# Turning eight half batches by transposing DMAs in a linear-attention and routed-MLP kernel

## The chip, the cores and the metric

The kernel runs on one core of one Trainium2 chip. The metric is the device time of that core in microseconds, the median of several runs. Before the change it is 963.09 us (three runs, 963.00 to 963.91). The profiled execution has a span of 960.4 us at a granted TensorE clock of 1.00.

## The reference

Two stages follow each other. Linear attention over 8 batches, 8 heads, 576 tokens and a head size of 64:

```python
q_p, k_p = phi(q), phi(k)                      # phi(x) = elu(x) + 1
kv  = einsum('bhsd,bhse->bhde', k_p, v)
z   = sum(k_p, axis=2)
num = einsum('bhsd,bhde->bhse', q_p, kv)
den = einsum('bhsd,bhd->bhs', q_p, z)[..., None] + 1e-6
x   = (num / den)                              # then laid out as 4608 tokens x 512
```

Then a routed MLP on x with 8 experts, hidden size 1024:

```python
P = exp(x @ w_gate);  eight times: normalise rows, then columns (Sinkhorn)
out = sum over e of  P[:, e:e+1] * (relu(x @ w1[e]) @ w2[e])
```

Every expert sees every token, so the two matmuls per expert are nearly all of the arithmetic.

## The kernel before

**Stages.** The front computes attention. The work is cut into 16 *half batches* n = 2b + g: batch b, four of its eight heads. The function `att(b, g)` makes the tasks of one. The result is `xT`, the attention output with features on the partitions and tokens along the free axis, as the first MLP layer needs it. The MLP is cut into units of 512 tokens (g = 0 to 8) per expert e. For expert 0, units 0 to 4 are plain (`layer1` at L583 for `hq`, `unit_plain` at L809 for `ye`), and units 5 to 8 have a first layer of seven block products instead of eight (`block7`, matmuls at L703). Experts 1 to 7 use seven-product forms for both layers (L703, L927). Those begin near 193 us and are the rest of the span.

**One half batch.** k, q and v come by DMA (L269). ScalarE takes the exponential (L285), VectorE makes phi in two steps (L298, L301) into the tile `t`, and v is cast to fp16 beside a column of ones (`f_v`, L229 or L231). TensorE forms k^T v and the sum of k in the PSUM tile `kv_ps` (18 matmuls, L330), whose buffer is single (`p_kv`). It is masked into `kvz` (L341 or L343). q is transposed by TensorE (`qt_ps`, L358) and copied (`qpT`). Then the denominators (`den_ps`, 10 small matmuls, L373), `rden` (an addition and a reciprocal, L379 and L381), the numerators (`num_ps`, L397), their product with the reciprocals (`xn`, three VectorE instructions, L402), two times five TensorE transposes (`xt_ps`, L413) and two copies of 128 x 576 from PSUM into `xT`. `qt_ps`, `den_ps`, `num_ps`, `xt_ps`, the gate's logits and one of the block products share the two PSUM buffers `att`. `xn` has two buffers.

**What waits for the front.** `logits` (L432) needs `xT` of two batches and starts the Sinkhorn rounds, whose P is first needed to finish unit 8 of expert 0. At the end of the front its SBUF and PSUM are closed (`f_close`) and given to what follows: the weight combinations `W` of `block7` (VectorE, L867), the blocks `xst` and the loads `xs` (L653). An instruction on the new tiles waits for the last reader of the old ones. Blocks of x are stored to DRAM for the later experts (`x_blocks`, stores at L606, L607, L636).

**What sets the order.** Every engine runs its instructions in program order. That order is made by the class `_Plan`, a list scheduler: each task has engines with a cost in us, dependences, buffers it takes and a priority, and is emitted when its planned start comes. The priorities are overwritten by a long table of ranks by task number (L1084 on), some of which also pin a task to an engine. A DMA is planned as a task on its issuing engine and one on a single `dma` engine, with a latency of 2.6 us after it. The front runs interleaved with the plain units of expert 0. At the very start 47 warm-up matmuls (L505) fill TensorE.

Of the kernel before, what the change touches and what calls it, by code (L numbers as in the profile page):

```python
# [10 lines left out]
FP32 = mybir.dt.float32  # L11
FP16 = mybir.dt.float16
# [110 lines left out]
def kernel(  # L123
# [10 lines left out]
    nc = tc.nc  # L134
# [34 lines left out]
    NX = 5  # L169
    MG = 99  # L170
# [19 lines left out]
    p_vv, p_kvz, p_qpT, p_xn, p_rden = (S_.pool(2) for _ in range(5))  # L190
# [47 lines left out]
    gates = {}  # L238
    v_land, kv_id = [], []
# [6 lines left out]
    def att(b, g):  # L246
# [67 lines left out]
        def f_v(e):  # L314
            copy(e, gvv["tile"][:, :, :, 0:D], gin["v"]["tile"])
        tvv.append(fadd({"act": 1.15, "dve": 0.76}, f_v, deps=[ta, tin["v"]],
                        use=[gvv, gin["v"]], prio=pr))
# [49 lines left out]
        gden, grd, gxn = S_.grp(p_att), S_.grp(p_rden), S_.grp(p_xn)  # L367

        def f_den(_):
            gden["tile"] = aps.tile([P, 5, 2, 2], FP32, tag="att", name="den_ps")  # L370
            for i, j in enumerate(js):
                for hh in range(2):
                    nc.tensor.matmul(gden["tile"][:, i, :, hh],  # L373
                                     lhsT=gq["tile"][:, hh, j:j + 2, :].rearrange("p j w -> p (j w)"),
                                     rhs=gz["tile"][:, hh, :, D], start=True, stop=True)

        def f_rd(_):
            grd["tile"] = fp.tile([P, 5, 4], FP32, tag="rden", name="rden")
            nc.vector.tensor_scalar(out=grd["tile"], in0=gden["tile"].rearrange("p i r h -> p i (r h)"),  # L379
                                    scalar1=1e-6, scalar2=None, op0=ALU.add)  # L380
            nc.vector.reciprocal(grd["tile"], grd["tile"])  # L381
        tden = fadd(("pe", 0.26), f_den, deps=tq + tz, acq=[gden], use=[gq, gz], prio=pr)
        trd = fadd(("dve", 0.5), f_rd, deps=[tden], acq=[grd], use=[gden], prio=pr)

        def f_xa(_):
            gxn["tile"] = fp.tile([P, 5, 4, D], FP16, tag="xn", name="xn")
        txa = fadd(("none", 0.0), f_xa, deps=[tden], acq=[gxn], prio=pr)
        txn = []
        for i0, i1 in ((0, 2), (2, 4), (4, 5)):
# [11 lines left out]
            def f_xn(_, i0=i0, i1=i1, gn=gn):  # L401
                nc.vector.tensor_tensor(  # L402
# [4 lines left out]
        for c2 in range(2):  # L407
            gx = S_.grp(p_att)

            def f_xt(_, c2=c2, gx=gx):  # L410
                gx["tile"] = aps.tile([P, S], FP16, tag="att", name="xt_ps")
                for i in range(5):
                    nc.tensor.transpose(gx["tile"][:, 64 * js[i]:64 * js[i] + P],  # L413
                                        gxn["tile"][:, i, 2 * c2:2 * c2 + 2, :].rearrange("p r e -> p (r e)"), ident)

            def f_xc(e, c2=c2, gx=gx):
                copy(e, xT[:, 2 * g + c2, S * b:S * b + S], gx["tile"])
            t1 = fadd(("pe", 0.3), f_xt, deps=txn, acq=[gx], use=[gxn], prio=pr)
            xt_done[(b, 2 * g + c2)] = fadd({"act": 0.64, "dve": 0.46}, f_xc, deps=[t1], use=[gx], prio=pr)
# [5 lines left out]
    def logits(b2):  # L425
# [11 lines left out]
        t1 = lg_pe[b2] = add(("pe", 1.0), f_l, deps=[xt_done[(b, c)] for b in (2 * b2, 2 * b2 + 1) for c in range(NDT)],  # L437
# [74 lines left out]
    for i in range(34):  # L512
        twa = add(("pe", 0.3), lambda e, n=2 if 4 <= i < 17 else 1: f_warm(e, n), deps=[twa], use=[gyw], prio=900.0, after=1.2 + 0.5 * i)
# [46 lines left out]
    def layer1(e, g):  # L560
        gw1, tw1, gw2, tw2 = w_t[e]
        bs = range(512 * g // S, (512 * g + 511) // S + 1)
        xd_ = [xt_done[(b, c)] for b in bs for c in range(NDT)]
# [34 lines left out]
    def x_blocks(g):  # L598
        bs = range(512 * g // S, (512 * g + 511) // S + 1)
        deps = [xt_done[(b, c)] for b in bs for c in range(NDT)]  # L600
# [420 lines left out]
    for tt in (3, 2, 1, 0):  # L1021
# [5 lines left out]
        0:-50.0024 36:8.7509 38:8.7566 40:-50.0207 42:-49.9982 43:8.7608 44:-50.0228 45:8.7578 46:-50.0192  # L1027
        47:-50.0138 49:8.7452:act 50:-49.9982 51:-50.0108 52:-50.0204:act 54:8.7572 55:-50.0216 56:8.7563
        57:-49.9985:act 58:-50.0222 59:-50.0213 61:-50.0117 62:-50.0036 63:-50.012 64:8.759 65:-50.0135
        66:-98.0291 67:-50.012 68:8.7602:dve 69:-49.9994 70:-50.0129:act 71:-50.015 73:-50.0144 75:-49.9886  # L1030
        77:-50.0129 78:-49.9988 79:-50.0186 80:8.7587 81:-50.0207 82:-50.0027 84:-50.0198 85:-49.9829
        86:-49.9985:act 88:-98.021 89:-50.015:act 90:-50.0201 91:8.7617:dve 92:-50.0195 93:-50.0219
        95:-50.0162 96:8.7575 97:-50.0201 98:-50.0186 99:8.7464 100:-98.0051 101:-50.0195 102:-50.0144:act
        103:-50.0141 104:-50.0198 106:8.7632 108:8.7575 110:-49.9844 112:-50.0216 114:-50.0006 116:8.7575
        117:-50.0132 118:-50.0006 119:-50.021 120:-50.0192 121:-49.9982 123:-50.0201:dve 124:-50.0159
        125:-50.0225:dve 127:-50.0138 128:-50.0105:dve 129:8.762 130:-50.0213 131:-98.0054 132:-50.0189
        134:-49.9787 135:-50.0207 136:-49.9859 137:-50.003 138:-50.0018 139:-50.0228 140:-50.0153
        141:-50.0093:dve 142:-49.9811 143:-50.0003:dve 144:-50.0156 146:-50.012 148:-50.0147 150:-50.0237
        151:-50.021 152:8.7593 153:-50.0204 154:-50.0192 155:-50.0156 157:-50.0003:act 158:-50.0159
        159:8.7368:dve 161:-50.0117 162:-50.0147:act 163:-50.0021 164:-50.0213 165:-50.0222 166:8.7443  # L1040
        168:-50.021 169:-50.0231 170:-50.0168 171:-50.0267 172:-50.0216 173:-50.0144 174:-50.0228
        175:-50.0228:dve 176:-50.0201 177:-49.9787:act 179:-50.0063 181:-50.006 183:-50.0144 184:-50.0189
        185:-50.0189 187:-50.0168 189:-50.0048 191:8.7584 192:-49.9802 193:-50.0225 194:-50.0255
        195:-50.0201 196:-50.0219 198:-50.0195 199:-50.0132 200:-50.0207:dve 202:-50.0249 203:-50.0144
        204:-50.0015 205:-50.0213:dve 206:-98.0237 207:-50.012 209:-50.0183 210:-50.0204 211:-50.0258
        212:-50.0288 213:-50.0189 214:-50.0237 215:-49.9808 216:-49.9856:act 217:-50.0219 218:-50.0117:dve
        219:8.7602 221:-50.0153 223:-49.9991 225:-50.0015 226:-50.0165 227:-50.0225 228:-50.0162
        229:-98.0078 230:-50.0165 232:-50.0087:dve 233:-98.0054 234:8.7512:dve 236:-50.0216 237:-98.0051:act
        238:-50.0246 239:-50.0165:dve 240:-50.0219 241:-98.0048 243:-50.027 244:-50.0195 245:-50.0135
        246:-50.0126 247:-50.0228 248:-50.0123 249:-50.0159 250:-50.018:act 251:-98.0228 252:-49.9826  # L1050
        253:-50.018 255:-50.0213 257:-50.018 259:-50.0162 260:-50.0231 261:-98.0063 262:-50.0282 263:-50.012
        264:-50.0003 266:-50.0117:dve 267:-50.0159 268:8.7464:act 270:-50.0195 271:8.7509:act 272:-98.0054
        273:-50.0168 274:-50.0162 275:-98.0246 277:-50.015 278:-50.0213 279:-50.0243 280:-50.0273
        281:-50.0174 282:-98.0231 283:-98.003 284:-50.0198:act 285:-98.0261 286:-50.0228:dve 287:-98.0048
        289:-49.9814 291:-49.9808 293:-50.0267 294:-49.9856 295:-50.0282 296:-50.0045 297:-50.0243
        298:8.7446 300:-49.9805 301:-50.0276 302:-50.0186:dve 304:-50.0204 305:-50.0123:act 306:-50.0132
        307:-98.006:act 308:-50.0207 309:-50.0219 311:-49.9784 312:-50.0192 313:-50.0189 314:-50.0123
        315:-50.021 316:-50.012 317:-49.9754 318:-50.0135 319:-50.0162 320:-49.9826:act 321:-50.0015
        322:-50.0249 323:-50.0126 325:-98.0048 327:-50.0198 329:-50.0108 330:-50.0174 331:8.7458 332:-49.985
        333:-50.0162 334:-50.0153 336:-50.0159:dve 337:-50.0171 338:-49.9793:dve 340:-98.0294 341:-98.033  # L1060
        342:-50.015 343:-49.9859:dve 344:-50.0165 345:-50.0156 347:-49.9823 348:-50.0141 349:-49.988
        350:-50.0216 351:-98.0258 352:-50.0177 353:-50.0096 354:-49.9853 355:-50.0171 356:-49.9835:dve
        357:-98.0282 359:-50.0234 361:-50.0138 363:-50.0117 364:-50.0228 365:-50.0168 366:-50.0147
        367:-49.982 368:-50.0126 370:8.7449:act 371:-49.9769 372:-50.0174:act 374:-49.9802 375:-98.0018:act
        376:-50.0231 377:-50.0168 378:-50.0186 379:-50.0108 381:-50.0114 382:-50.0114 383:-50.0174
        384:-50.0222 385:-50.0261 386:-98.0051 387:-50.0021 388:-50.012:act 389:-50.0258 390:-50.0093:dve
        391:-50.0114 393:-50.0138 395:-49.9814 397:-49.9853 398:-50.0192 399:-49.9847 400:-50.009
        401:-50.0207 402:8.7413 404:-49.9781:act 405:8.7524 406:-50.0102:dve 408:-50.0225 409:-50.0006:dve
# [132 lines left out]
```

The softmax here doesn't subtract the row's maximum and nothing guards it: scores larger than these inputs give would overflow.

## Time and profile before

| | value |
|---|---|
| median time, range | 963.09 us, 963.00 to 963.91 |
| span of the profiled execution | 960.4 us |
| TensorE busy | 954.2 us (99%) |
| VectorE, ScalarE busy | 773.4 us (81%), 572.4 us (60%) |
| TensorE busy from 0 to 20 us | 18.58 us, warm-up included |
| last transpose of the front (`xt_ps`) | starts at 127.1 us |
| first seven-product unit of an expert after the first | about 193 us |

The page divides the span into busy time of engines, and then into groups of instructions by line. Matmuls are pipelined and their ends are modelled, so the mean duration of one is longer than the distance to the next: the chain of work, in which neighbours don't overlap, shows what a row of matmuls really takes. PE is TensorE, PEld its weight load, DVE is VectorE, ACT ScalarE, POOL GpSimd, SP the sync engine, whose only work is to issue DMAs.

### The profile page before, as it was taken

What the parts mean: (1) busy time and instruction counts of PE and PEld (TensorE: products, weight loads), DVE (VectorE), ACT (ScalarE), POOL (GpSimd) and SP (SyncE); (2) the same over time, 40 slices, a digit from 0 to 9 for tenths busy, and PEclk for the clock granted to TensorE, in tenths of its full rate; (3) what the DMA queues carried; (4) which work ended last, traced back from release to release, by engine and by line L of the source; (5) the groups of instructions that cost most, each with busy time, mean ns of one, the idle gap of its engine ahead of it and who ended that gap; (6) DMA issues with size and microseconds to landing.
All of it is one profiled execution on the core that took longest, in us unless ns stands there. A gap on an engine that the chain in (4) does not pass through costs nothing.

```text
span 960.4 us, 21585 instructions
## 1 busy us (share of the span) xinstructions
PE 954.2 (99%) x8833; PEld 803.7 (84%) x8833; DVE 773.4 (81%) x1527; ACT 572.4 (60%) x1034; POOL 114.1 (12%) x163
## 2 busy tenths in 40 slices
PE   9999999999999999999999999999999999999998
PEld 4666676688888888888888888888888888888886
DVE  6998889878887888878887888878887888877775
ACT  6897755855555555555555555555555555555553
POOL 4100000011111111111111100111111111111110
PEclk9999999999999999999999999999999999999999
DMA  9987962252227222452227222272226321235554
GB/s 317 345 315 259 277 195 77 44 122 78 78 77 165 78 77 78 113 130 77 78 78 164 79 78 78 81 162 74 68 71 136 93 78 74 78 100 164 166 162 114
DMA packets 46420, 121.99 MB, mean 127 GB/s; under 512 B 4208, under 2 KB 18288, under 8 KB 46320
## 3 DMA queue, kind: packets, MB, share of 16 engines
q1 hardware_dynamic: 30576, 96.22, 30.1%
q0 software_dynamic: 15344, 23.87, 12.9%
q8 instruction: 69, 1.13, 0.5%
q10 hardware_dynamic: 400, 0.52, 0.2%
q14 instruction: 31, 0.25, 0.1%
HBM read 119.69 MB, written 17.69 MB: 143 GB/s over the span
## 4 chain that ended last, share of the span: by engine, by line
PE 95%; DMA 2%; ACT 2%; DVE 0%; issue 0%; POOL 0%; ACTq 0%; DVEq 0%
PE ye L927 34%; PE hq L703 24%; PE att L703 12%; PE ye L809 7%; PE Zye L703 6%; PE Zye L927 6%; PE hq L583 3%; DMA kqin<-in_k_dram 2%; ACT e L285 1%; PE xt_ps L413 1%; PE kv_ps L330 1%; PE num_ps L397 1%; PE qt_ps L358 1%; ACT h L587 0%; PE lg_ps L432 0%; PE den_ps L373 0%
## 5 line engine op out<-in xcount | busy, mean ns | idle before, releaser
L941 DVE SCALAR_TENSOR_TENSOR acc<-ye,P_sb,acc 128x256 f32<-128x256 f32 x620 | 267.3, 479 | 128.1 <-PE ye L927 127.6
L703 PEld LDWEIGHTS <-W 128*128 128x128 f16 x2144 | 209.8, 98 | 26.8 <-issue 0.2
L927 PEld LDWEIGHTS <-S 128*128 128x128 f16 x1984 | 194.1, 98 | 22.5
L927 PE MATMUL ye<-T,S 128*128 128x256 f16 x1488 | 192.8, 273 | 0.0
L703 PEld LDWEIGHTS <-w 128*128 128x128 f16 x1608 | 157.4, 98 | 20.1 <-issue 0.7
L735 ACT ACTIVATE h<-hq 128x512 f16<-128x512 f32 x134 | 80.1, 597 | 146.2 <-PE hq L703 143.3
L951 POOL TENSOR_TENSOR acc<-acc,st 128x256 f32<-128x256 f32 x124 | 87.3, 724 | 619.9 <-ACT st L948 609.2
L927 PEld LDWEIGHTS <-h 128*128 128x128 f16 x1488 | 145.6, 98 | 16.8
L703 PE MATMUL att<-xs,W 128*128 128x256 f16 x1008 | 151.2, 273 | 0.0
L703 PE MATMUL hq<-xs,W 128*128 128x256 f16 x1008 | 151.2, 273 | 0.0
L703 PE MATMUL hq<-xs,w 128*128 128x256 f16 x1008 | 140.9, 273 | 0.3 <-DVE h L738 0.3
L732 ACT ACTIVATE h<-Zye 128x512 f16<-128x512 f32 x134 | 80.1, 598 | 42.6 <-PE Zye L703 42.6
L948 ACT ACTIVATE st<-Zye,P_sb 128x256 f32<-128x256 f32 x124 | 51.9, 470 | 78.0 <-PE Zye L927 78.0
L900 DVE TENSOR_TENSOR S<-h 128x1024 f16<-128x1024 f16 x124 | 85.4, 689 | 13.7 <-ACT h L735 13.7
L738 DVE CUSTOM_DVE_ANT_0 h<-att,s 128x512 f16<-128x512 f32 x126 | 86.7, 688 | 11.7 <-ACT s L722 11.1
L722 ACT COPY s<-hq 128x512 f32<-128x512 f32 x126 | 73.6, 584 | 36.3 <-PE hq L703 36.3
L715 ACT COPY Zye<-hq 128x512 f32<-128x512 f32 x134 | 78.0, 582 | 17.8 <-PE hq L703 17.7
L738 DVE CUSTOM_DVE_ANT_0 h<-hq,s 128x512 f16<-128x512 f32 x126 | 86.7, 688 | 0.6 <-PE hq L703 0.6
L809 PE MATMUL ye<-w,h 128*128 128x512 f16 x312 | 76.6, 379 | 0.0
L703 PE MATMUL Zye<-xs,w 128*128 128x256 f16 x504 | 75.6, 273 | 0.0
L729 ACT COPY s<-att 128x512 f32<-128x512 f32 x126 | 74.6, 592 | 0.0
L927 PE MATMUL ye<-w,h 128*128 128x256 f16 x496 | 64.3, 273 | 0.0
(109 smaller groups left out, 949.7 us busy)
## 6 DMA issues: line engine op xcount, KB each, us to landing
xs<-xd SPq DMA_DIRECT2D x63, 896.0 KB, 4.6
w<-in_moe_w_dram POOLq DMA_DIRECT2D x14, 1024.0 KB, 11.5
out_dram<-acc SPq DMA_DIRECT2D x67, 128.0 KB, 2.4
kqin<-in_k_dram SPq DMA_DIRECT2D x12, 576.0 KB, 5.2
kqin<-in_q_dram SPq DMA_DIRECT2D x12, 576.0 KB, 6.6
vin<-in_v_dram SPq DMA_DIRECT2D x12, 576.0 KB, 7.3
xd<-acc SPq DMA_DIRECT2D x5, 512.0 KB, 4.9
kqin<-in_k_dram POOLq DMA_DIRECT2D x4, 576.0 KB, 10.5
```

The costliest lines, as they stand in the source:

```text
L703: nc.tensor.matmul(dst[:, p, :], lhsT=lhs(p, c), rhs=rhs(c), start=(first and p == 0 and c == 0), stop=(c == 1), skip_group_check=True)
L715: nc.scalar.copy(out=Zt[1], in_=gX["tile"])
L722: nc.scalar.copy(out=gs2["tile"], in_=gX["tile"])
L729: nc.scalar.copy(out=gs5["tile"], in_=gR["tile"])
L732: nc.scalar.activation(out=hd(0, 0), in_=Zt[1], func=AF.Relu)
L735: nc.scalar.activation(out=hd(1, 0), in_=gX["tile"], func=AF.Relu)
L738: nc.vector._custom_dve(TENSOR_ADD_SAT, out=dst, in0=ps, in1=sb, s0=3.0e38, s1=0.0)
L809: nc.tensor.matmul(gy[tt]["tile"], lhsT=gh["tile"][:, f, ds(P * tt, P)], rhs=gw2["tile"][:, f, :], start=(f == 0), stop=(f == NFT - 1))
L900: nc.vector.tensor_tensor(out=Sx[:, i], in0=a0, in1=a1, op=op)
L927: nc.tensor.matmul(bank(g_)[:, s, :], lhsT=lhs(s, kk), rhs=rhs(kk), start=(new and s == 0 and kk == 0), stop=(kk == 3), skip_group_check=True)
L941: nc.vector.scalar_tensor_tensor(out=dst(), in0=bank(g_)[:, s, :], scalar=P_sb[:, gg, e:e + 1], in1=dst(), op0=ALU.mult, op1=ALU.add)
L951: nc.gpsimd.tensor_tensor(out=dst(), in0=dst(), in1=gst["tile"], op=ALU.add)
```

## The change

**Transposing DMAs.** For the half batches n = 8 to 15 (`DX = 8`) the ten TensorE transposes and two PSUM copies go. Instead the sync engine issues three transposing DMAs from `xn` straight into `xT`: one of 128 x 512 for each of the two feature blocks, and one of 64 x 256 for the last 64 tokens of both. `xn` is laid out for it, so the three VectorE instructions write another pattern. The planner gives the sync engine 1.2, 1.2 and 0.6 us for the issues and the transfers 0.6, 0.6 and 0.2 us plus the latency.

**Denominators.** They are written to spare columns of the first bank of `kv_ps` instead of a buffer of `att`. The constant `ND` is 16, so this holds for all sixteen half batches. The next half batch's k^T v then waits for `rden` of this one, as `kv_ps` has one buffer.

**The start.** For n = 0 and 1 the last 64 tokens are transposed and copied apart, so that the first 512 tokens need two of the three `xn` instructions. The cast of v for n = 1 is cut in two, which two engines can share. Three warm-up matmuls fewer.

**Order.** The table of ranks (`ranks`, some 80 lines) is new as a whole, since the tasks are renumbered; it is left out below.

The aim is to take work off TensorE, and pressure off the `att` buffers and the two engines that empty PSUM. Cut to its core:

```diff
+    ND = 16
+    SPX = 1.2
+    DX = 8
-        def f_v(e):
-            copy(e, gvv["tile"][:, :, :, 0:D], gin["v"]["tile"])
+        for r0, r1 in ((0, 1), (1, 2)) if n == 1 else ((0, 2),):
+            def f_v(e, r0=r0, r1=r1):
+                copy(e, gvv["tile"][:, r0:r1, :, 0:D], gin["v"]["tile"][:, r0:r1])
...
-        gden, grd, gxn = S_.grp(p_att), S_.grp(p_rden), S_.grp(p_xn)
+        gden, grd, gxn = gkv if n < ND else S_.grp(p_att), S_.grp(p_rden), S_.grp(p_xn)
...
+            if n < ND:
+                dent.append(gkv["tile"][:, 0, 256:276].rearrange("p (i r h) -> p i r h", i=5, r=2))
...
-        for c2 in range(2):
-            gx = S_.grp(p_att)
-            def f_xt(_, c2=c2, gx=gx):
-                gx["tile"] = aps.tile([P, S], FP16, tag="att", name="xt_ps")
-                for i in range(5):
-                    nc.tensor.transpose(gx["tile"][:, 64 * js[i]:64 * js[i] + P],
-                                        gxn["tile"][:, i, 2 * c2:2 * c2 + 2, :].rearrange("p r e -> p (r e)"), ident)
-            def f_xc(e, c2=c2, gx=gx):
-                copy(e, xT[:, 2 * g + c2, S * b:S * b + S], gx["tile"])
+        if n >= DX:
+            td = []
+            for c2 in range(3):
+                def f_xd(_, c2=c2):
+                    if c2 < 2:
+                        nc.sync.dma_start_transpose(
+                            out=xT[:, 2 * g + c2, S * b:S * b + 512].rearrange("p (i t) -> p i t", t=P),
+                            in_=gxn["tile"][:, c2, 0:4].rearrange("p i r e -> p (i r e)"))
+                    else:
+                        nc.sync.dma_start_transpose(
+                            out=xT[:, 2 * g:2 * g + 2, S * b + 512:S * b + S],
+                            in_=gxn["tail"][64:P].rearrange("p c r e -> p (c r e)"))
+                ti = fadd(("sp", SPX if c2 < 2 else 0.6), f_xd, deps=txn[0:2] if c2 < 2 else [txn[2]], use=[gxn], prio=pr)
+                td.append(fadd(("dma", 0.6 if c2 < 2 else 0.2), lambda _: None, deps=[ti], use=[gxn], prio=pr, lat=2.6))
+        else:
+            ni = 4 if n < 2 else 5
+            ni = 4 if n < 2 else 5
...
+                t1 = fadd(("pe", 0.06 * ni), f_xt, deps=txn if ni == 5 else txn[0:2], acq=[gx], use=[gxn], prio=pr)
...
+            if ni == 4:
+                gx = S_.grp(p_att)
...
-    for i in range(34):
+    for i in range(31):
...
     ranks = """
...
```

## The prediction, made before the run

> **What bounds the kernel.** I read the page's first part, then the stretches of 20 us, then the chain of waits around the end of the front, then what the sync engine waits for and the timeline of the start. First the page:
>
> ```profile
> PE 954.2 (99%) x8833; PEld 803.7 (84%) x8833; DVE 773.4 (81%) x1527; ACT 572.4 (60%) x1034; POOL 114.1 (12%) x163
> ```
>
> TensorE is busy 99% of the span, so nothing but its work and its waits can move the end. The stretches (us, then busy us of PE, PEld, DVE, ACT, POOL, clock, DMA share, GB/s) say whether any part has slack:
>
> ```profile
> 20.00:40.00 20.00, 19.73 (x215) 11.82 (x214) 17.79 (x35) 16.60 (x24) 4.98 (x7) 1.00 1.12 342
> 40.00:60.00 20.00, 20.00 (x232) 12.19 (x229) 19.26 (x38) 18.51 (x27) 0.00 (x0) 1.00 0.95 352
> 80.00:100.00 20.00, 19.68 (x253) 12.87 (x251) 17.51 (x37) 16.54 (x26) 0.00 (x0) 1.00 0.95 322
> 100.00:128.00 28.00, 28.00 (x328) 17.93 (x326) 21.43 (x49) 18.62 (x34) 2.09 (x3) 1.00 0.88 220
> ```
>
> From 20 us on TensorE has no idle stretch; in the front VectorE, ScalarE and the DMAs are nearly full as well. After 193 us the change touches no computation, so a gain must come from the first 193 us: less TensorE work, an earlier start of the solid stream, or fewer small waits. The chain of work at the end of the front (start, us, what) gives the real price of a row of transposes and what stands behind it:
>
> ```profile
> 126.74 0.56 PE xt_ps L413 x10
> 127.30 0.86 PE ye L809 x4
> 128.16 0.88 PE lg_ps L432 x36
> 129.05 0.45 PE Zye L551 x2
> 129.50 1.73 PE ye L809 x8
> 131.22 0.87 PE hq L703 x8
> ```
>
> Ten transposes take 0.56 us. After the last of them TensorE has 3.92 us of other work (127.30 to 131.22) until the first product of `block7`. What that product's companions need, the combinations `W`, starts on VectorE as soon as the front's buffers are free, and so do the loads `xs`. The sync engine's waits, 60 to 140 us (total, times, longest), show what it was waiting for:
>
> ```profile
> SPq L653 <- PE xt_ps L413: 0.9, 1, 0.9
> ```
>
> And the timeline shows both starting within 0.4 us of the last transpose's end (127.36):
>
> ```profile
> 127.43 1.41 SPq L653 DMA_DIRECT2D xs<-xd  x2
> 127.71 0.68 DVE L867 TENSOR_TENSOR W<-w 128x1024 f16<-128x1024 f16 x1
> ```
>
> The last transpose is the event that opens the next stage. In the new kernel the landing of the last transposing DMA takes its place.
>
> **What the Trainium skill says.** "VectorE: DVE Perf Modes", section "The three transpose paths", gives 390 ns for a 128 x 128 transpose on TensorE and 1309 ns by DMA. The trace differs on the first: in a row they cost 56 ns each; no run here shows the second. "DMA: Bandwidth & Descriptors", section "Latency and other measured facts", gives 261 GB/s for transposing DMAs with a strided pattern, by which 128 KB would move in an estimated 0.5 us. No run here shows it. The same page, section "Issuing engines are not separate DMA queues", says that DMAs from all engines share the 16 DMA engines and interleave. The trace agrees: a 512 KB store (L636) landed 2.7 us after its issue at 75.69 us, but 8.6 us after the issue at 112.36 us, when two weight loads were under way (issued at 107.20 and 108.23, landed after 11.7 and 17.1 us).
>
> **The change part by part.**
>
> *Transposes removed.* Eight half batches x 10 transposes = 8 x 0.56 = 4.5 us less TensorE work, all on the path, since the stream is solid. The 16 copies removed (0.455 us on VectorE or 0.639 us on ScalarE, half of them on each) free some 8.8 us over two engines that don't bound the end; alone they are worth nothing, but they let attention run earlier. The `xn` instructions (0.68 and 0.41 us) keep their size. I take the new pattern at the same price.
>
> *Transposing DMAs.* Issue: between 0.48 us (the shortest plain issue at L607) and 1.27 us (the longest); the planner's 1.2, 1.2 and 0.6 are at the upper end and I take them: 3.0 us of the sync engine per half batch. A half batch has 108/16 = 6.7 us in the front, so the sync engine isn't the bound. Queued behind a transposing DMA that waits for `xn` are loads of later half batches and stores of x blocks. n = 15's v landed at 106.9 us and was needed at 118.5 us by k^T v, so a load may be late by some us. Transfer: landing 2.7 us (the undisturbed store) to 8.6 us (the store beside the weight loads) after the issue. From the last `xn` to the landing of the tail that is 0.6 + 2.7 = 3.3 to 0.6 + 8.6 = 9.2 us. Before, it took 1.1 us (the last `xn` ends at 126.33, the loads go at 127.43). So the opening event comes 2.2 to 8.1 us later after `xn`.
>
> *Is that hidden?* To gain in full, `W` must open earlier by what TensorE saves, 4.5 us and the 0.9 us of the start below: 5.4 us. So attention must be brought forward by 7.6 to 13.5 us. Room: between 108 and 127 us twelve rows of four `ye` matmuls (0.86 us each) stand among attention's; put behind it they give 10.3 us. The last half batch takes from 106.9 us (v landed) to 126.3 us (`xn` done), 19.4 us, for a chain that in the start takes 6.3 us (the cast of v begins at 12.78, the third `xn` ends at 19.07): its own dependences allow 10.3 us. So the wait that remains is 0 to 3.2 us. The weight loads end near 125 us, and the last transposing DMAs are issued in that window's second half, so I take a third of the upper end, 1.1 us. The new order has the task of making this room; it costs nothing itself.
>
> *Denominators in `kv_ps`.* Same matmuls, same reads, one user of `att` fewer. The wait added: k^T v of n + 1 stands behind `rden` of n, two VectorE instructions of 0.17 + 0.28 us after the denominators, and since TensorE runs in order all its work is queued behind a k^T v that waits. In the old order k^T v of n = 15 started at 118.50, before `rden` of n = 14 was done at 119.2. With a row of `ye` between the two (0.86 us) it is hidden: 0 us. If it never were, 16 x some 0.5 us = 8 us; I keep that for the slow side.
>
> *The start.* Its timeline:
>
> ```profile
> 12.78 1.16 ACT L229 CAST vv<-vin 128x1152 f16<-128x1152 f32 x1
> 15.25 0.63 ACT L341 ACTIVATE kvz<-kv_ps,half 128x130 f16<-128x130 f32 x2 [0.16 <-PE kv_ps L330]
> 15.84 0.46 DVE L231 COPY xT<-xt_ps 128x576 f16<-128x576 f16 x1 [0.19 <-PE xt_ps L413]
> 16.41 0.41 PE L373 MATMUL den_ps<-kvz,qpT 128*128 128x2 f16 x10
> 17.45 1.62 DVE L402 TENSOR_TENSOR xn<-num_ps,rden 128x512 f16<-128x512 f32 x3
> 19.95 2.31 PE L583 MATMUL hq<-xT,w 128*128 128x512 f16 x9
> ```
>
> The cast of n = 1 cut in two saves up to 0.5 us (1.16 against the planner's 0.64). The denominators waited for an `att` buffer until the copy ended at 16.30, although `kvz` was ready at 15.88: 0.4 us. The transposes no longer wait for the third `xn`: 0.4 us. Together up to 1.3 us by which the solid stream (19.95) starts earlier. But the next data don't come earlier: v of n = 2 landed at 22.7 us and the last part of w2 at 32.2 us, and the DMAs are full until 60 us. I take 0.9 us, with 0 and 1.3 as ends. The three warm-up matmuls removed are filler. The small tail transposes and copies add some 0.2 us to engines with room.
>
> Sum: 963.1 - 4.5 - 0.9 + 1.1 = 958.8 us.
>
> **Rivals.**
>
> *All hidden, and fewer small waits* (chance 0.11). The DMAs land in time, the start gives 1.3 us and some of the front's small waits go (transposes waited 0.3 us for the exponential of the logits, which held an `att` buffer): 963.1 - 4.5 - 1.3 - 0.7 = 956.6 us (0.7 an estimate: two waits of such a size). For it: a half batch takes an `att` buffer eight times now, and five times from n = 8 on. Against it: full DMAs until 60 us.
>
> *The gain is eaten at the end of the front* (0.15). The last transposes land beside the weight loads, 8 us late, and the start gives nothing: 963.1 - 4.5 + 3.2 = 961.8, up to 963.5 with small waits for `rden`; I place it at 962.5 us. For it: the 8.6 to 12.3 us that stores took at 112 us. Against it: the stores of 76 us took 2.7 to 4.0 us.
>
> *Slower* (0.15). A transposing DMA of 128 x 512 holds its queue for 3 us and not 0.6: a half batch then needs 2 x 3 + 1.2 = 7.2 us against 6.7 us, 4 us more over eight, and loads wait behind it in the sync engine's order. On top of the late landing: 963.1 - 5.4 + 3.2 + 4 = 964.9 us. With the skill's 1309 ns per 128 x 128, one after the other, a half batch takes 11.8 us and the front ends some 40 us late, near 1000 us. k^T v waiting for `rden` adds up to 8 us. I place this case at 966 us. Against the far end: 16 DMA engines should work on one at a time.
>
> *The forecast case* has the rest, 0.59.
>
> **How the numbers follow.** 958.8 us is the likeliest case. Below 956.0 I leave 0.05. Above 965.0 I leave 0.12, most of the slow case. Faster by over 0.2% means under 961.2 us: the forecast case, the all-hidden case and a third of the eaten one, 0.59 + 0.11 + 0.05 = 0.75. Within 0.2%: 0.10. Slower: 0.15.
>
> **What would show it.** Right: the `xt_ps` group falls from 160 to about 80 matmuls; the first solid `hq` row starts near 19 us; the first `block7` product near 126 us; after that the trace runs as before, 5 us or so earlier; `W` starts right after a landing. Wrong: TensorE idle between 118 and 132 us with `W` or the logits waiting for a DMA into `xT`; transposing DMAs that land over 9 us after their issue; idle time before k^T v released by `rden`; the exponentials waiting for loads issued late.

## The result, and the profile after

The kernel after takes 975.99 us (median of four runs, 975.04 to 976.34) against 963.50 us for the kernel before beside it. The ratio is 1.0125 with a 95% interval of 1.0108 to 1.0143: the change costs 12.5 us, where a saving of 4.3 us was forecast.

First the row of TensorE on the page of the kernel after, with the count of DMA packets and the queue of the sync engine:

```profile
PE 954.0 (98%) x8750; PEld 800.4 (82%) x8750; DVE 771.5 (79%) x1521; ACT 566.7 (58%) x1030; POOL 114.0 (12%) x163
...
DMA packets 56403, 124.34 MB, mean 128 GB/s; under 512 B 14192, under 2 KB 28272, under 8 KB 56304
...
q1 hardware_dynamic: 40560, 98.58, 31.7%
```

83 matmuls are gone (8833 to 8750: 80 transposes and three of the warm-up), yet TensorE is busy 954.0 us as before, in a span of 973.2 us. Some of the matmuls must have become slower, and some 13 us of idle time is new. Each large DMA of the change moved 128 KB in 512 packets of 256 bytes: the page of before counted 46420 packets, this one 56403.

The stretches of the kernel after show where it is (us, then busy us of PE, PEld, DVE, ACT, POOL, granted clock, DMA share, GB/s):

```profile
20.00:40.00 20.00, 19.06 (x197) 11.22 (x195) 16.80 (x33) 15.14 (x23) 4.83 (x7) 1.00 1.11 339
40.00:60.00 20.00, 20.00 (x197) 12.02 (x196) 17.32 (x33) 19.07 (x31) 0.00 (x0) 1.00 0.96 337
...
80.00:100.00 20.00, 17.65 (x218) 10.60 (x215) 17.16 (x37) 14.45 (x22) 0.00 (x0) 1.00 1.10 318
100.00:120.00 20.00, 16.25 (x198) 10.26 (x193) 13.29 (x27) 14.92 (x25) 1.83 (x3) 0.91 1.07 231
120.00:141.00 21.00, 15.30 (x99) 7.84 (x98) 7.85 (x20) 4.16 (x8) 0.00 (x0) 0.84 1.00 206
```

Up to 60 us little has changed: TensorE is busy 0.7 us less from 20 to 40 us, and as much from 40 to 60 us. In the last three it idles 2.4, 3.7 and 5.7 us, where it was all but solid before, and its clock falls to 0.91 and 0.84. The DMA share is 1.10 where it was 0.95 (the times of all packets are added up, so overlapping ones can take it past 1). Two shorter stretches of the same view hold the slow clock:

```profile
103.00:107.00 4.00, 3.83 (x18) 2.07 (x18) 1.96 (x4) 3.27 (x7) 0.00 (x0) 0.57 1.04 237
128.00:134.00 6.00, 6.00 (x48) 3.41 (x48) 2.42 (x6) 1.11 (x3) 0.00 (x0) 0.50 1.22 247
```

A row of four matmuls of 512 columns takes 1.91 us there (at 131.56 us) and 1.03 us elsewhere (at 118.31 us). The chain of work around the end of the front, which was a row of TensorE pieces before, is now a row of transfers (start, us, what; pieces between are left out):

```profile
87.42 4.92 DMA kqin<-in_k_dram
...
99.29 8.79 DMA kqin<-in_k_dram
...
115.90 11.23 DMA xT<-xn
127.21 0.70 DVE xn L420
127.95 0.37 PE num_ps L413 x2
...
136.99 1.26 SPq L437
138.35 2.29 DMA xT<-xn
140.76 0.43 DVE xst L678
```

Three kinds of delay are in it: loads of k issued late or slow (87.42, 99.29), a transposing DMA that took 11.23 us and held an `xn` buffer until it had landed (115.90), and the landing that opens the next stage (140.6 us; the last transpose ended at 127.30 us before). The timeline has what waited for them:

```profile
101.38 1.16 ACT L290 ACTIVATE e<-kqin 128x1152 f16<-128x1152 f32 x1 [3.46 <-DMA kqin<-in_k_dram]
...
103.08 1.70 PE L641 MATMUL hq<-xT,w 128*128 128x512 f16 x4 [2.93 <-ACT h L645]
...
127.21 0.69 DVE L420 TENSOR_TENSOR xn<-num_ps,rden 128x512 f16<-128x512 f32 x1 [5.28 <-DMA xT<-xn]
...
127.95 0.37 PE L413 MATMUL num_ps<-kvz,qpT 128*128 128x128 f16 x2 [4.97 <-DVE xn L420]
...
140.76 0.43 DVE L678 TENSOR_TENSOR xst<-xT 128x512 f16<-128x512 f16 x1 [4.13 <-DMA xT<-xn]
```

At 101 us an exponential waits for a load, a relu (`h`) stands behind it on ScalarE, and TensorE waits for the relu, 2.9 us. From 123 to 128 us TensorE waits 5.0 us for `xn`, which waits for a buffer that a DMA still reads. And the two lines of the transposing DMAs (duration of the issue in ns min/median/max, first and last start; then who waited, and the time to landing), the 128 x 512 ones and the tails:

```profile
L437 SPq DMA_TRANSPOSE xT<-xn x16: 1196/1518/3480, 79.9 to 137.0; - x16
...
DMA to landing us min/median/max: 2.5/5.4/11.2
```

```profile
L441 SPq DMA_TRANSPOSE xT<-xn x8: 1163/1178/1315, 81.3 to 138.4; - x8
...
  DVE xn L420: 5.3, 1
  DVE xst L678: 4.1, 1
...
DMA to landing us min/median/max: 2.3/6.4/11.2
```

**Where the loss lies.** A comparison of the same work serves for the rest of this document. It leaves the warm-up and the transposes of x out of both traces and asks at each time by how much the changed kernel is ahead of the kernel before (minus: behind), counted in us of the latter. A change that only took the transposes out would end at +4.5. The figures are good to about half a microsecond, since they depend on the price given to each kind of matmul.

```
at us      24     65     80     90    100    105    120    130    140    205
after    -0.4   +0.1   +0.2   +0.9   -0.8   -4.5   -5.2  -10.8  -12.0  -12.8
```

All of it is lost between 92 and 140 us: against the +4.5 of an undisturbed change, 17.4 us from 65 us on.

### The profile page after: what moved, and what is told of

Its sections match the earlier page's. It is cut to its first block, busy times and chain, and to the rows that moved or that the text cites. A ratio compares the mean times of both kernels' runs of the same rounds, so it can differ in the third digit from the quotient of the medians.

```text
span 973.2 us, 21452 instructions
## 1 busy us (share of the span) xinstructions
PE 954.0 (98%) x8750; PEld 800.4 (82%) x8750; DVE 771.5 (79%) x1521; ACT 566.7 (58%) x1030; POOL 114.0 (12%) x163
## 4 chain that ended last, share of the span: by engine, by line
PE 89%; DMA 5%; ACT 2%; DVE 2%; SPq 1%; issue 0%; DVEq 0%; ACTq 0%
PE ye L985 33%; PE hq L761 24%; PE att L761 12%; PE Zye L761 6%; PE Zye L985 6%; PE ye L867 5%; DMA kqin<-in_q_dram 3%; PE hq L641 2%; DMA kqin<-in_k_dram 1%; DMA xT<-xn 1%; ACT e L290 1%; PE num_ps L413 1%; PE kv_ps L336 1%; PE qt_ps L364 0%; SPq L274 0%
## 5 line engine op out<-in xcount | busy, mean ns | idle before, releaser
L985 PE MATMUL ye<-w,S 128*128 128x256 f16 x496 | 64.3, 273 | 0.0
```

Of the source, the lines that this page charges most:

```text
L985: nc.tensor.matmul(bank(g_)[:, s, :], lhsT=lhs(s, kk), rhs=rhs(kk), start=(new and s == 0 and kk == 0), stop=(kk == 3), skip_group_check=True)
```

## Experiments

In all of them the kernel before ran beside, at 963.6 to 964.4 us. Those named e_ change the kernel after, those named b_ the kernel before; each keeps its kernel's order of instructions but for what the text says is moved.

**TensorE transposes in the new order.** The body of each transposing DMA is replaced:

```diff
+ px = aps.tile([P, 512], FP16, tag="att", name="xt_ps")
+ nc.tensor.transpose(px[...], gxn["tile"][:, c2, i]..., ident)   # four, or two for the tail
+ copy(("act", "dve")[c2], xT[...], px)
- nc.sync.dma_start_transpose(...)
```

> The changed kernel, every instruction in its order, but at the place of each transposing DMA of n = 8 to 15 stand the TensorE transposes and a copy from PSUM again (80 transposes, 24 copies). Theory Q (the transposing DMAs are the cause: their issue fills the sync engine, loads come late, and their landing holds the xn buffers): 961 to 966 us, as before the change. Rival O (the new order, or the denominators in kv_ps, are the cause): 970 us or more.

972.70 us, 1.0088 (1.0071 to 1.0105), in the range given to rival O. With 4.5 us of transposes put back it is 3.3 us faster than the kernel after. It is not a clean undo: the transposes take an `att` buffer again that the order doesn't plan, and TensorE waits up to 0.8 us at a time for it. It says that the DMAs cost more than they save, and that this kernel without them is no gain either; how much of that is the new order's, and how much the unplanned `att` buffer's, it doesn't tell.

**Loads from the GpSimd queue, and from ScalarE's.** One word each, for the k, q and v of n = 12 to 15:

```diff
- (nc.gpsimd if 2 <= n <= 5 else nc.sync).dma_start(
+ (nc.gpsimd if 2 <= n <= 5 or n >= 12 else nc.sync).dma_start(                        # e_pool
+ (nc.gpsimd if 2 <= n <= 5 else nc.scalar if n >= 12 else nc.sync).dma_start(         # e_actq
```

> The changed kernel, but q, k and v of n = 12 to 15 are loaded from GpSimd's queue, so that no load stands behind a transposing DMA on the sync engine. Theory Q: the waits for late loads between 92 and 110 us go (some 6 us with the slow clock after them), those for xn at 122 us stay: 968 to 971 us. Rival C (only the landing beside the weight loads counts): 974 us or more.

> The changed kernel, but q, k and v of n = 12 to 15 are issued from ScalarE's queue, which is a hardware queue as the sync engine's is. Theory I (the issues of transposing DMAs fill the sync engine from 79 to 110 us, so loads are issued late): the loss of 5.5 us between 92 and 110 us goes: 969 to 972 us. If loads from any other queue starve the transposing DMAs, as those from GpSimd did in e_pool: 980 us or more.

994.77 us (1.0320, 1.0304 to 1.0335) and 981.52 us (1.0185, 1.0170 to 1.0200). Freeing the sync engine of loads made both worse. In e_pool the waits of TensorE (total, times, longest) name the transposing DMA itself, and its landings reach 23.7 us:

```profile
PE hq L641 <- DMA xT<-xn: 13.1, 1, 13.1
PE ye L867 <- ACT h L645: 7.0, 1, 7.0
PE lg_ps L490 <- DMA xT<-xn: 5.4, 2, 3.6
```

In e_actq a load's issue blocks ScalarE until 93.4 us, and `xn` waits for its buffer again, with TensorE behind it:

```profile
PE num_ps L413 <- DVE xn L420: 9.4, 3, 7.3
PE kv_ps L384 <- ACT qpT L233: 5.9, 1, 5.9
```

So the place in the sync engine's order isn't all of it: with the loads on another queue, transposing DMAs landed up to 23.7 us (e_pool) and 13.7 us (e_actq) after their issue, where the most in the kernel after was 11.2 us.

**The weight loads of expert 1 later.** GpSimd reads a column of `xT` ahead of the two issues, so that they come behind the tail of n = 15 (e_wlate), or behind the landings of both last half batches (e_wlast):

```diff
+ nc.gpsimd.tensor_copy(out=gate[...], in_=xT[:, ..., N - 2:N])   # waits for transposing DMAs
  fn(_)                                                            # the weight load
```

> The changed kernel, but the two weight loads of expert 1 are issued behind the last transposing DMA and wait for its landing. Rival C: the wait of 5.1 us at 122.6 us and the slow clock after it go, and no other wait remains of note: 964 to 967 us. Theory Q: that wait goes, those for late loads stay: 967 to 971 us. If the landing is slow by itself: 974 us or more.

> The changed kernel, but the two weight loads of expert 1 are issued behind every transposing DMA and wait for all of their landings (in e_wlate one half batch came after them). Theory B (beside loads from GpSimd's queue a transposing DMA lands late, and holds its xn buffer): landings after 112 us fall to 2.5 to 4 us, the wait of 5.1 us and the slow clock after it go: 967 to 970 us. If landing late isn't the cause of that wait: 974 us or more.

985.61 us (1.0223, 1.0208 to 1.0239) and 983.26 us (1.0199, 1.0183 to 1.0214). In e_wlate the loads fell upon the last transposing DMAs, which landed up to 17.9 us after their issue; TensorE waited twice for them:

```profile
PE lg_ps L511 <- DMA xT<-xn: 15.2, 2, 9.8
```

In e_wlast the landings are quick, as expected of theory B. The 128 x 512 DMAs between 112 and 145 us, first in the kernel after, then in e_wlast:

```profile
DMA to landing us min/median/max: 2.5/6.5/11.2
...
DMA to landing us min/median/max: 2.4/2.5/4.0
```

So the late landings of the kernel after from 112 us on are due to the weight loads beside them. The 5-us wait for `xn` is gone too (at 135 us it is 6.1 us behind, the kernel after 12.4), but then the weights come late, and more than the gain is paid back:

```profile
DVE W L947 <- DMA w<-in_moe_w_dram: 10.0, 1, 10.0
```

Neither is a way out: in e_wlast the weights landed at 156 and 164 us, and TensorE stood for 9.3 us at 156 us.

**The same bytes without turning.** Plain DMAs of the same size at the same places; the x of n = 8 to 15 isn't turned, so those tokens of x are not the reference's.

```diff
- nc.sync.dma_start_transpose(
-     out=xT[:, 2 * g + c2, S * b:S * b + 512].rearrange("p (i t) -> p i t", t=P),
+ nc.sync.dma_start(
+     out=xT[:, 2 * g + c2, S * b:S * b + 512],
```

> The changed kernel, but the 24 transposing DMAs are plain DMAs of the same bytes from xn to xT (x isn't transposed: that part of the computation is left out). If the price is that of transposing, in issue and transfer: issues near 0.5 us and 958 to 964 us. If any three more DMAs per half batch on this queue cost it: 970 us or more.

968.15 us (1.0044, 1.0029 to 1.0059): 7.8 us less than the kernel after, between the two ranges expected. Its issue takes a median of 0.57 us and not 1.52, and its packets are 1024 bytes at 46 ns and not four times 256 bytes at 18 ns undisturbed, 27 ns on the mean from 76 to 112 us:

```profile
L437 SPq DMA_DIRECT2D xT<-xn x16: 465/565/1232, 80.7 to 130.6; - x16
```

**No transposing DMAs, and tiny ones.** e_none leaves the DMAs out (the x of n = 8 to 15 is set to zero early by GpSimd); e_tiny keeps all 24 at their places, but each turns only 16 x 128 numbers (the rest of that x is zero).

```diff
+ nc.gpsimd.memset(xT[:, c, 4 * S:N], 0.0)          # both, once
- nc.sync.dma_start_transpose(...)                   # e_none
+ nc.sync.dma_start_transpose(out=xT[:, ..., t0:t0 + 16], in_=gxn["tile"][0:16, c2, 0]...)   # e_tiny
```

> The changed kernel without its 24 transposing DMAs: x of n = 8 to 15 is zero, set by GpSimd early in the front; all else in its order. Theory D (the DMA engines, already full from 76 to 112 us, are loaded with some 17 us of 256-byte packets, and loads and landings are late for that): all losses go, 957 to 961 us. Rival O (the new order itself loses): 966 us or more.

> The changed kernel with its 24 transposing DMAs at their places and with their waits, but each moves 16 x 128 elements and no more (16 packets and not 512 or 128; the rest of x of n = 8 to 15 is zero). Theory D: near e_none, at most 963 us. Theory I (their issue and their waits on the sync engine delay the loads, whatever they move): 968 us or more.

967.90 us (1.0038, 1.0025 to 1.0051) and 972.95 us (1.0090, 1.0075 to 1.0105), as they stand in the ranges of rival O and of theory I. But both are some 4 us behind at 60 us already. This is put down to the memset, an artefact: it runs from 31 to 39 us, and beside it a VectorE instruction that takes 0.75 us elsewhere took 4.09 us, after which TensorE waits 2.6 us for `xn`.

```profile
35.29 4.09 DVE L306 TENSOR_SCALAR t<-kqin 128x1152 f16<-128x1152 f32 x1
```

So only what follows 65 us is compared. As both start there 4 to 5 us late, their waits for loads are not quite what they would be on time, and the split is a rough one:

```
lead at us   65     80    100    120    140    205     lost from 65 on, against +4.5
e_none     -3.7   -3.7   -4.4   -4.5   -4.8   -4.8      1.1 + 4.5 =  5.6
e_tiny     -4.7   -4.7   -6.6   -9.9   -8.9  -11.2      6.5 + 4.5 = 11.0
after      +0.1   +0.2   -0.8   -5.2  -12.0  -12.8     12.9 + 4.5 = 17.4
```

Even with no DMA at all the new order loses 5.6 us to waits, with the exponentials and `h` behind the loads of k as in the kernel after (total, times, longest):

```profile
ACT e L293 <- DMA kqin<-in_k_dram: 3.7, 2, 2.4
```

The step to e_tiny, the issues and waits of the DMAs, adds some 5.4 us, and the step to their full packets some 6.4 us. The issue of a tiny one costs as much as the shortest of a large one:

```profile
L440 SPq DMA_TRANSPOSE xT<-xn x24: 1085/1218/2059, 84.4 to 137.3; - x24
...
DMA to landing us min/median/max: 2.3/5.3/8.7
```

and the sync engine then waits for `xn` ahead of loads that could go (total, times, longest):

```profile
SPq L440 <- DVE xn L423: 6.4, 4, 3.1
```

**Stores out of the way, more `xn` buffers, both.** The stores of the x blocks of units 0 to 4 behind the last transposing DMA (e_rawlate), four `xn` buffers from n = 8 on, three of them in `acc5`, which is written after the front only (e_xn4), and the two together:

```diff
+ if early: S_.late.add(ti)        # e_rawlate: stores are emitted after the last transposing DMA
- xn_ = fp.tile([P, 5 * 4 * D], FP16, tag="xn", name="xn", bufs=2)
+ xn_ = (fp.tile(...) if k_ == 3 else acc[5]...[:, 1280 * k_:1280 * k_ + 1280])   # e_xn4, k_ = (n - DX) % 4
```

> The changed kernel, but the stores of the raw x blocks of units 0 to 4 (384 KB each, 5 us of all DMA engines between 76 and 130 us) are issued behind the last transposing DMA. Theory D: the loads and landings get that time back, 970 to 973 us. Theory I: four DMAs fewer before 110 us on the sync engine, each 0.5 us, 974 us. Theory B alone: 976 us.

> The changed kernel with four buffers of xn for n = 8 to 15 and not two. If the late landing at 127.1 us counts because it holds an xn buffer: the wait of 5.1 us at 122.6 us and the slow clock after it go, 968 to 971 us. If the landings are late for what follows anyway (logits, the end of the front): 974 to 977 us.

> The kernel after with both the raw stores of units 0 to 4 behind the last transposing DMA (alone 3.1 us faster) and four xn buffers (alone 2.5 us faster). If the two are separate causes: 976 - 3.1 - 2.5 = 970.4 us. If both only hand the same waiting on to the landing of the last transposes: 972 to 973 us. The kernel before stays the fastest, 963.5 us, in both.

972.86, 973.45 and 972.72 us (ratios 1.0093, 1.0094 and 1.0082, with intervals of 0.0022 or less to each side): 3.1 and 2.5 us each, but 3.3 together by the medians. In e_xn4 the 5-us wait for `xn` has gone, and the next one has come in its place:

```profile
PE lg_ps L492 <- DMA xT<-acc: 3.5, 3, 2.4
```

This speaks for causes that overlap: what one frees waits for the next landing. It isn't shown, though. The times of both together lie between 970.65 and 973.94 us, and 970.4 us, which two separate gains would give, is still within the interval of the ratio.

**The denominators back in `att`.**

```diff
- if n < ND:
+ if False:
```

> The kernel after in its own order, with only the denominators back in a buffer of att instead of the spare columns of kv_ps. If the single kv_ps buffer, held until rden is made, is what leaves the 5.6 us of waits without transposing DMAs: 970 to 973 us. If the order is (theory): within 1.5 us of after, 974.5 to 977.5 us, or slower, since the order was made for one user of att less.

979.20 us (1.0156, 1.0140 to 1.0172), 3.2 us slower than the kernel after. TensorE then waits for `rden` 2.2 us and for `P_sb` 0.7 us, which it doesn't after. The move to `kv_ps` is worth 3.2 us in this order, which was made for it, and the 5.6 us aren't its.

**Only the DMAs, in the order of before.** The new layout of `xn` and the DMAs for some half batches; the planner's costs and so the order stay:

```diff
+ XD = (8, 9, 10, 11, 12, 13, 14, 15)    # b_dma8_15; (8, 9, 10, 11): b_dma8_11; (6, 7): b_dma6_7
+ if n in XD:
+     nc.sync.dma_start_transpose(...)   # where the TensorE transposes stood
+     return
```

> The kernel before in its own order, with one part of the change alone: n = 8 to 15 are turned by the three transposing DMAs, at the places where the TensorE transposes stood. Rival O (the new order is at fault, the DMAs are not): 958 to 963 us. Theories B and I (the DMAs are at fault in any order): 967 us or more.

> The same for n = 8 to 11 alone, whose transposing DMAs come before the weight loads and are needed late. TensorE saves 4 x 0.56 = 2.2 us. Theory B alone: 960 to 962 us. Theory I (their issue delays the loads of n = 13 to 15): 964 us or more.

984.94 us (1.0212, 1.0193 to 1.0231) and 973.15 us (1.0091, 1.0076 to 1.0106). The waits of TensorE in b_dma8_15:

```profile
PE num_ps L403 <- DVE xn L410: 8.2, 1, 8.2
PE lg_ps L458 <- DMA xT<-xn: 4.4, 4, 1.6
PE lg_ps L458 <- DVE rden L380: 3.4, 1, 3.4
PE den_ps L374 <- ACT kvz L342: 3.1, 1, 3.1
```

The DMAs alone cost 21 us. In b_dma8_15 the sync engine was issuing for 28.6 us between 79 and 111 us, where it was 9.7 us before, and the loads of n = 13 to 15 were issued 2.4 to 7.7 us later, in the same order of tasks. The new order, the denominators and the start took 9 us of the loss back: they did make room, but not enough.

**Two half batches, and the delays taken away one by one.** The `xn` of n = 6 and 7 is done by 71 us, and in the kernel before the DMA share is only 0.25 from 72 to 78 us.

> The kernel before with its own order; only the x of n = 6 and 7 is turned by transposing DMAs (20 TensorE transposes less, 20 x 56 ns = 1.1 us). Their xn is done between 62 and 71 us; the DMA engines fall to a share of 0.25 between 72 and 78 us. Theory (it loses because the DMA engines are full and loads stand behind): here there is room right after, so the gain shows: 962.2 to 963.5 us, no wait over 0.5 us between 60 and 80 us. Rival (a transposing DMA costs its users a late landing or an xn buffer wherever it is put): 965 us or more, with TensorE waiting for xn or for a DMA into xT near 66 to 76 us.

968.51 us (1.0047, 1.0031 to 1.0063). The first theory missed: room on the DMA engines right after isn't enough. The timeline shows two other delays:

```profile
74.69 0.42 DVE L417 TENSOR_TENSOR xn<-num_ps,rden 128x256 f16<-128x256 f32 x1 [2.32 <-DMA xT<-xn]
...
83.19 1.47 SPq L427 DMA_TRANSPOSE xT<-xn  x1
...
88.08 0.66 PE L609 MATMUL hq<-xT,w 128*128 128x512 f16 x2 [2.25 <-DMA xT<-xn]
```

The `xn` of n = 8 waits for the DMA that reads its buffer (issued at 70.13 us behind others, landed at 74.56). The last of the six DMAs stands behind six stores on the sync engine; its `xn` was done at 71.36 us, it was issued at 83.19, and TensorE waited 2.25 us. After this the clock was low until 95 us, which cost another 2.0 us:

```profile
91.00:95.00 4.00, 4.00 (x34) 2.58 (x33) 2.99 (x5) 1.54 (x4) 0.00 (x0) 0.50 1.04 384
```

So the two were taken away one after the other: `xn` of n = 6 and 7 in `acc5`, then also the six stores behind the last DMA.

```diff
+ xn_ = acc[5]...[:, 1280 * (n - 6):1280 * (n - 6) + 1280] if n in XD else fp.tile(...)   # b_dma6_7_xn4
+ if early: S_.late.add(ti)    # b_dma6_7_late as well: stores behind the last DMA of n = 7
```

> b_dma6_7 with the xn of n = 6 and 7 in memory of their own (in acc5, which is written after the front only), so that no later xn waits for a transposing DMA to have read its buffer. If that wait is one cause: the waits of TensorE at 71.2, 74.9 and 77.9 us (0.6 + 0.8 + 0.9 us) go, 966.0 to 967.0 us instead of 968.5; the 2.4 us before the last transposing DMA and the slow matmuls after it stay. If buffers don't matter: 968 to 969 us.

> The same, and the six stores of x blocks that stood ahead of the last transposing DMA of n = 7 on the sync engine put behind it (otherwise the order is kept). If the sync engine's order is the other cause: the 2.4 us wait and the slow matmuls after it (2.0 us) go too, and the saving of 20 transposes shows: 962.5 to 963.7 us, level with the kernel before or up to 1.1 us faster. If a transposing DMA loses by something else: 965 us or more.

965.60 us (1.0026, 1.0016 to 1.0035), then 962.93 us (0.9990, 0.9981 to 0.9999), which is in the range expected. By the medians the first step took 2.9 us off where 1.5 to 2.5 were expected (some 0.7 us of it by less slow clock; 2.0 us by the ratios), the second 2.7 (some 1.4 us of it by the clock). In the last kernel the DMA that stood behind the stores goes at 74.67 us, and TensorE waits for no landing and no `xn` between 66 and 92 us:

```profile
74.67 1.93 SPq L440 DMA_TRANSPOSE xT<-acc  x1
```

The 20 transposes saved are worth 1.1 us by 20 x 56 ns; 0.7 us of it is seen, with an interval from 0.1 to 1.8 us. This is the only version that is faster than the kernel before, by 0.1%. The moved stores and the separate memory were not tried without the DMAs. But the kernel before had little idle time to lose there: 0.32 of these 26 us, against 0.80 in this version (the first line is the kernel before):

```profile
66.00:92.00 26.00, 25.68 (x286) 16.36 (x286) 21.79 (x48) 20.97 (x35) 0.00 (x0) 1.00 0.79 281
66.00:92.00 26.00, 25.20 (x273) 15.54 (x270) 21.75 (x48) 19.94 (x33) 0.00 (x0) 1.00 1.02 306
```

## Why the prediction was wrong

**Right.** *Transposes removed*: the 80 matmuls went, and TensorE's work with them. *Denominators in `kv_ps`* at 0 us: no wait of k^T v for `rden` shows in the kernel after, and e_den has the move on the good side by 3.2 us, more than the 0 allowed. *What would show it wrong* listed mechanisms that came: TensorE idle at 118 to 132 us (by way of `xn`, though, and not of `W` or the logits), landings over 9 us (11.2), exponentials that wait for loads issued late.

**The step that failed first: "so the sync engine isn't the bound".** The working compared 3.0 us of issue with 6.7 us for a half batch, a mean. The issue was taken too small: the shortest of a large one costs 1.2 us as taken, but the tail costs that as well (1.18, not 0.6), and a large one up to 3.5 us when others are under way, so that a half batch took 4.7 us on the mean. That is still under 6.7 us; the failure is that a mean says nothing of the order. From 79 to 111 us the sync engine was issuing for 28.7 of 32 us, and an instruction that waits for `xn` keeps the loads behind it. The loads of n = 13 to 15 were issued 1.6 to 7.5 us later than before; the new order has a part in this, but in b_dma8_15, with the order of before, it was 2.4 to 7.7 us. e_tiny beside e_none puts this part at some 5.4 us; b_dma6_7_late beside b_dma6_7_xn4 shows the reverse case, stores ahead of a DMA, at 2.7 us.

**The transfer was charged no DMA time.** The prediction saw the DMA share of 0.95 at 80 to 100 us and took only latency from it. Between 76 and 112 us the 256-byte packets take 6.7 us of all 16 engines (3970 packets x 27 ns / 16 engines), and a load packet of 2304 bytes grew from 103 to 114 ns beside them. There was no room for it: after less e_tiny is some 6.4 us, of which 2.9 us are slower matmuls (3.9 us of slow clock in after, 1.0 in e_tiny after 65 us). e_plain shows the price of turning more directly: the same bytes, not turned, cost 7.8 us less, issue and packets together.

**"Is that hidden?" looked at one event, the landing that opens `W`, and gave it 1.1 us.** It came 13 us later than before, not hidden. The room for it was counted too large as well: between 108 and 127 us the kernel before has ten rows of four `ye` matmuls, 8.6 us, and not twelve. What the step missed is that the source is held as well: with TensorE an `xn` buffer was free when the transposes had read it, with the DMA only when it has landed, 2.3 to 11.2 us after the issue. Two buffers then stop VectorE, and through `num_ps` TensorE: 5.0 us at 123 us. b_dma6_7 and b_dma6_7_xn4 show this term, 2.9 us with the slow clock in it. The 8.6-us store beside the weight loads was the right warning, as e_wlast shows, and the range of 2.7 to 8.6 us too short: it was 2.3 to 11.2.

**"It costs nothing itself"** was said of the new order. Without any DMA it loses some 5.6 us (e_none), and not by the denominators (e_den). That the remaining waits come from loads of k and the order in which exponentials and `h` stand on ScalarE is read from the trace, not tried.

**The start** was put at 0.9 us. Its lead of 0.6 us at 20 us is gone at 24 us, where TensorE waits for phi of n = 2, whose q landed at 21.3 us. That was the lower end given, 0, for the reason given.

**A cost that no step had: the clock after a wait.** Many waits of TensorE were followed by a stretch at half clock. In the kernel after it began 3 to 4 us after the wait did and cost 3.9 us in all (1.5 behind the wait at 100 us, 2.4 behind that at 123 us). Length alone doesn't decide: TensorE stood for 3.1 us from 89.1 us in b_dma8_15 and from 89.9 us in b_dma8_11, and only the second was followed by half clock (0.50, the figure before the DMA share):

```profile
92.20:99.00 6.80, 6.71 (x74) 3.94 (x74) 6.36 (x16) 6.80 (x9) 0.00 (x0) 1.00 1.26 292
93.00:96.00 3.00, 2.92 (x22) 1.76 (x22) 1.99 (x7) 2.59 (x5) 0.00 (x0) 0.50 1.04 389
```

The clock records of the traces say why this may be. Between 20 and 900 us every half-clock stretch of every run lasts 3.41 us or a whole multiple of it, and within a run the starts lie whole multiples of 3.41 us apart (103.28 and 127.17 us in the kernel after: seven). In b_dma8_11 the 3.41 us before its stretch, from 89.48 us, were nearly all idle; on the grid of b_dma8_15 the wait falls across two such windows. So where a wait falls seems to count beside its length; no run moved a wait to try it.

The forecast's rival *slower*, 966 us, had the place (loads behind the DMAs in the sync engine's order), but a size of 4 us for it. Sum of what the runs show, from 65 us on: -4.5 for the transposes, +5.6 order, +5.4 issue and order of the sync engine, +6.4 packets and the slow clock behind them = +12.9 us, beside 12.5 us measured. It closes because each part is a difference of neighbours in one row. The causes may well overlap, as e_xn4 and e_rawlate together suggest, so that this is a split by the order of taking away, not one of independent parts. What stays open is how all eight half batches would do in an order planned with these costs; that wasn't tried.

## What to carry to other kernels

Before moving an on-chip step from an engine to a DMA, list what the DMA holds and for how long: its source buffer until landing, its place in the issuing engine's order with the loads and stores around it, and engine time on the DMAs in that very stretch, not on average. The two half batches showed that such a move pays only when both the source buffer and the place in the order are given room; the gain is then no more than the matmuls saved, 0.7 us, while either one that is missing cost 2 to 3 us. In a kernel whose TensorE is solid, allow for slow clock behind each new wait of 2 us or more: where it came in the kernel after, it cost another 1.5 and 2.4 us.

## What was not expected of the hardware

- A transposing DMA occupies the sync engine for 1.2 us whatever it moves (1.22 us for 16 x 128, 1.2 us at least for 128 x 512), where a plain DMA of the same bytes took 0.57 us.
- Landing: 2.3 to 2.5 us after the issue for both sizes when undisturbed. The Trainium skill ("DMA: Bandwidth & Descriptors", "Latency and other measured facts") gives 261 GB/s for a transposing DMA with strided pattern; its 256-byte packets took 18 ns here when undisturbed, 16 engines x 256 B / 18 ns = 228 GB/s, an estimate which is near, and 27 ns on the mean from 76 to 112 us, 152 GB/s. Beside loads from the GpSimd queue a landing took up to 17.9 us (e_wlate) and 23.7 us (e_pool).
- The slow clock. "TensorE: Matmul & The Clock Gate", Part 1, says that TensorE falls to half clock after an idle window of some 3.4 us and recovers after as much busy time. The traces agree on the half clock (0.50, with 0.43 us for 512 columns) and on the length: all its stretches between 20 and 900 us last 3.41 us or a multiple. It came after shorter waits than that, too: in b_dma6_7_xn4 after waits of 1.4 and 0.3 us, 3 us apart.
